# Output stores on another queue, preparation one step further ahead, and a hand-ordered start, in a RetNet-and-ELU kernel

## The chip, the cores and the metric

The kernel runs on one core of a Trainium2 chip. The metric is the device time of one launch in microseconds (us), the median of several executions. Engines in the views: PE (TensorE matmul), PEld (its weight loads), DVE (VectorE), ACT (ScalarE), POOL (GpSimd) and SP (SyncE, which here only issues DMAs). "SPq", "ACTq" and "POOLq" are the queues in which these engines issue DMAs. "PEclk" is the granted PE clock, 1.00 being full speed.

## The reference, cut to what matters

```python
# retention: batch 8, heads 8, sequence 576, head dimension 64
scores = (q @ k.T) / sqrt(64)
Dmat = where(rel >= 0, gamma_h ** rel, 0)      # rel = row - column, one gamma per head
x = ((scores * Dmat) @ v)                      # -> (4608 tokens, 512)
# feed-forward: 512 -> 2048 -> 512
h = x @ w_in
g = where(h > 0, h, exp(min(h, 0)) - 1)        # ELU
out = g @ w_out                                # (4608, 512) float32
```

## The kernel before

Retention works on tiles of 128 rows (and one of 64 at the end of each sequence). A tile is *loaded* (three DMAs: q, k, v), *cast* to bf16 with its decay factors, *turned* (q and k transposed, by PE in the early part and by a DMA transpose later), and put through scores, mask, products and state. The feed-forward part works on nine groups of 512 tokens: `ffn1` makes blocks of hidden units, `ffn2` multiplies them by `w_out`. An instruction given to `pin` keeps its place in program order; one given to `soft` is only pinned while `early[0]` is true.

```python
opool = ctx.enter_context(tc.tile_pool(name="opool", bufs=3))
ps_h  = ctx.enter_context(tc.tile_pool(name="ps_h", bufs=3, space=PSUM))
# ...
    # cast of a full tile, beyond the first batch: both on GpSimd
    soft(nc.gpsimd.tensor_tensor(qkn, rqk, g, ALU.mult))        # 128 x 1024, 1.9 us
    soft(nc.gpsimd.tensor_copy(vn, rv))                         # 128 x 512,  0.6 us
# ...
def ffn1(g, ft, lo=0, n=TG, relu=False):
    # ... four matmuls into ph, a PSUM buffer of ps_h ...
    soft(nc.scalar.activation(e[:, :n], ph[:, :n], AF.Exp))
    if relu:
        soft(nc.scalar.activation(em[:, :n], ph[:, :n], AF.Relu))
        soft(nc.vector.scalar_tensor_tensor(dst, e[:, :n], -1.0, em[:, :n], ALU.add, ALU.min))
    else:
        soft(nc.vector.tensor_scalar_add(em[:, :n], e[:, :n], -1.0))
        soft(nc.vector.scalar_tensor_tensor(dst, ph[:, :n], 0.0, em[:, :n], ALU.max, ALU.min))

def ffn2(g, it, fts, ...):
    # ... when the output tile is complete:
    ot = opool.tile([P, DM], FP32, name="ot", tag="ot")
    soft(nc.scalar.copy(ot, pm))
    pin(nc.sync.dma_start(out[i0 : i0 + P, :], ot))             # behind all loads and transposes on SP

def step():
    s = nxt[0]; nxt[0] += 1
    stretch(s); load(s + 4); cast(s + 2); turn(s + 1)
# ...
for ft in range(NFT):                                           # first 192 tokens of group 1
    ffn1(1, ft, 0, 192)
```

Note the two ways to make the ELU. Without `relu` VectorE runs a `tensor_scalar` (SBUF to SBUF) and a product whose inputs are PSUM and SBUF; with `relu` it runs one product with both inputs in SBUF, and ScalarE does the rest.

## Time and profile before

The time before is 358.93 us in the runs that the prediction had before it. The stage table of the prediction cuts the span at the program's seams:

| stage | what runs | us |
|---|---|---|
| S1, S2 | first tiles; weights arrive; group 0, first half of its outputs | 47.6 |
| S3 | rest of group 0, chains of tiles 4 and 5 | 17.8 |
| S4 | first 192 tokens of group 1 | 16.3 |
| S5 | two chains of tiles | 9.7 |
| S6 | rest of group 1, group 2 begins | 58.3 |
| S7 | steady state | 190.2 |
| S8 | last four output tiles | 17.7 |

### The profile page before, as it was taken

To read this page: it belongs to the slowest core of one execution; us is meant where nothing else is said; L and a number is where in the kernel's file an instruction comes from. 1 tells how busy PE (TensorE), PEld (TensorE's weight loads), DVE (VectorE), ACT (ScalarE), POOL (GpSimd) and SP (SyncE) were. 2 spreads that over 40 slices of the span, in tenths; PEclk is the share of its full clock that TensorE was granted. 3 is DMA by queue.
4 is the path that set the end of the run, shared out by engine and by line. 5 is a ranking of instruction groups with operands and counts; after the bars stand their busy time and mean duration, and the time that the engine had idled before them with its cause. 6 is when DMAs were issued, how large, how long until landed. Compare 5 with 4: busy or idle time off the path is not lost.

```text
span 357.6 us, 6117 instructions
## 1 busy us (share of the span) xinstructions
PE 313.9 (88%) x2319; PEld 161.7 (45%) x2319; DVE 236.3 (66%) x392; ACT 165.7 (46%) x331; POOL 107.1 (30%) x110
## 2 busy tenths in 40 slices
PE   2598983678677995999999999999998999999995
PEld 1443442565444442445444444445544454444442
DVE  3549920675769694967877877778878676666600
ACT  3468511434544562544554555454644455443411
POOL 4356366330255433521332444212234000000000
PEclk9999999559969998999999999999999999999999
DMA  9999999920999959796986896758879320010012
GB/s 172 227 335 332 277 212 232 201 45 18 203 199 199 197 119 205 140 169 141 177 168 136 179 203 132 170 123 186 169 158 140 73 47 29 29 60 29 29 70 78
DMA packets 151484, 53.74 MB, mean 150 GB/s; under 512 B 142752, under 2 KB 142752, under 8 KB 151456
## 3 DMA queue, kind: packets, MB, share of 16 engines
q1 hardware_dynamic: 151456, 53.36, 71.0%
q8 instruction: 18, 0.29, 0.4%
q14 instruction: 10, 0.08, 0.1%
HBM read 36.70 MB, written 9.44 MB: 129 GB/s over the span
## 4 chain that ended last, share of the span: by engine, by line
PE 65%; SPq 12%; DMA 10%; DVE 5%; ACT 4%; issue 2%; POOL 1%; ACTq 0%; POOLq 0%; DVEq 0%
PE pm L71 28%; PE ph L71 27%; SPq L169 10%; DMA qkT<-qkn 6%; PE o L71 4%; PE sc L71 3%; DMA rqk<-in_k_dram 3%; DVE em L324 2%; PE ptr L208 1%; ACT ot L335 1%; SPq L211 1%; DMA out_dram<-ot 1%; DVE g L325 1%; ACT qkT L209 1%; DVE pt L225 1%
## 5 line engine op out<-in xcount | busy, mean ns | idle before, releaser
L71 PE MATMUL ph<-xt,w_in_sb 128*128 128x512 bf16 (+2 forms) x640 | 153.5, 374 | 7.6 <-DVE g L325 5.8
L71 PE MATMUL pm<-w_out_sb,g 128*128 128x512 bf16 x576 | 144.4, 380 | 1.2 <-ACT ot L335 1.1
L317 ACT ACTIVATE e<-ph 128x512 f32<-128x512 f32 (+2 forms) x160 | 88.4, 555 | 93.4 <-PE ph L71 90.1
L324 DVE TENSOR_SCALAR em<-e 128x512 bf16<-128x512 f32 (+2 forms) x156 | 85.8, 552 | 60.7 <-ACT e L317 59.8
L325 DVE SCALAR_TENSOR_TENSOR g<-ph,em 128x512 bf16<-128x512 f32 (+2 forms) x156 | 98.9, 636 | 6.0
L71 PEld LDWEIGHTS <-w_in_sb 128*128 128x128 bf16 x640 | 63.5, 103 | 69.7 <-issue 11.0
L186 POOL TENSOR_TENSOR qkn<-rqk,gtab 128x1024 bf16<-128x1024 f32 x28 | 53.6, 1913 | 118.9 <-DMA rqk<-in_k_dram 92.3
L71 PEld LDWEIGHTS <-g 128*128 128x128 bf16 x576 | 56.4, 98 | 69.4 <-issue 3.2
L225 DVE TENSOR_TENSOR pt<-sc,mask 128x1024 bf16<-128x1024 f32 x32 | 38.9, 1217 | 20.0 <-PE sc L71 20.0
L262 ACT CAST xt<-o 128x512 bf16<-128x512 f32 (+1 forms) x44 | 21.9, 508 | 46.0 <-PE o L71 45.9
L335 ACT COPY ot<-pm 128x512 f32<-128x512 f32 x36 | 21.0, 586 | 34.8 <-PE pm L71 25.2
L71 PE MATMUL sc<-qkT 64*128 64x128 bf16 (+1 forms) x320 | 16.5, 228 | 20.7 <-DMA qkT<-qkn 10.6
L71 PEld LDWEIGHTS <-qkT 64*128 64x128 bf16 x320 | 9.4, 100 | 28.1 <-DMA qkT<-qkn 12.4
L187 POOL CAST vn<-rv 128x512 bf16<-128x512 f32 x28 | 20.0, 713 | 1.5 <-DMA rv<-in_v_dram 1.4
L208 PE MATMUL ptr<-ident,qkn 128*128 128x128 bf16 x64 | 7.1, 270 | 9.0 <-DVE qkn L182 8.0
L71 PE MATMUL o<-pt,vn 128*64 128x128 bf16 x256 | 14.1, 236 | 0.8 <-DVE pt L225 0.8
L192 POOL TENSOR_TENSOR qkt<-rqk,gtab 128x512 bf16<-128x512 f32 x8 | 8.3, 1042 | 21.0 <-DMA rqk<-in_k_dram 21.0
L209 DVE COPY qkT<-ptr 128x512 bf16<-128x512 bf16 x9 | 3.8, 425 | 14.0 <-PE ptr L208 14.0
L143 POOL CAST w_in_sb<-wst 128x512 bf16<-128x512 f32 x13 | 8.9, 689 | 5.9 <-DMA wst<-in_moe_w_in_dram 5.7
L208 PEld LDWEIGHTS <-qkn 128*128 128x128 bf16 x64 | 5.5, 122 | 11.2 <-DVE qkn L182 8.9
L71 PEld LDWEIGHTS <-vn 128*64 128x64 bf16 x256 | 8.7, 115 | 4.1 <-DVE pt L225 0.9
L71 PE MATMUL st<-vn,qkn 128*64 128x64 bf16 x256 | 10.2, 206 | 0.0
(59 smaller groups left out, 113.0 us busy)
## 6 DMA issues: line engine op xcount, KB each, us to landing
out_dram<-ot SPq DMA_DIRECT2D x36, 256.0 KB, 2.2
rqk<-in_q_dram SPq DMA_DIRECT2D x32, 256.0 KB, 4.0
rqk<-in_k_dram SPq DMA_DIRECT2D x32, 256.0 KB, 4.6
rv<-in_v_dram SPq DMA_DIRECT2D x32, 256.0 KB, 4.9
wst<-in_moe_w_in_dram SPq DMA_DIRECT2D x16, 256.0 KB, 5.3
wst<-in_moe_w_out_dram SPq DMA_DIRECT2D x16, 256.0 KB, 5.4
rqk<-in_q_dram SPq DMA_DIRECT2D x8, 128.0 KB, 3.1
rqk<-in_k_dram SPq DMA_DIRECT2D x8, 128.0 KB, 3.5
```

The costliest lines, as they stand in the source:

```text
L71: pin(nc.tensor.matmul(*a, **kw))
L143: soft(engines[eng](w_in_sb[:, j, n * 512 : (n + 1) * 512], t))
L169: pin(nc.sync.dma_start(dst, src[b, :, rows, :].rearrange("h p d -> p h d")))
L186: soft(nc.gpsimd.tensor_tensor(qkn, rqk, g, ALU.mult))
L187: soft(nc.gpsimd.tensor_copy(vn, rv))
L208: pin(nc.tensor.transpose(p[:, hp], flat[:, (i * HP + hp) * P : (i * HP + hp + 1) * P], ident))
L225: soft(nc.vector.tensor_tensor(pt.rearrange("p i h n -> p (i h) n") if n == P else pt, sc.rearrange("p i (h n) -> p (i h) n", h=HP) if n = ...
L262: soft(nc.scalar.copy(xt_tile(g)[:, :, off : off + w], o[:, :, c : c + w]))
L317: soft(nc.scalar.activation(e[:, :n], ph[:, :n], AF.Exp))
L324: soft(nc.vector.tensor_scalar_add(em[:, :n], e[:, :n], -1.0))
L325: soft(nc.vector.scalar_tensor_tensor(dst, ph[:, :n], 0.0, em[:, :n], ALU.max, ALU.min))
L335: soft(nc.scalar.copy(ot, pm))
```

## The change

The intent: loads and transposes should no longer stand behind a store that waits for its output tile; tiles should be prepared earlier; the start should lose the idle time between its chains. The core of the diff:

```diff
-opool = ... bufs=3
+opool = ... bufs=4
 # ffn2
-            pin(nc.sync.dma_start(out[i0 : i0 + P, :], ot))
+            soft(nc.gpsimd.dma_start(out[i0 : i0 + P, :], ot))
 # step
-        load(s + 4)
-        cast(s + 2)
-        turn(s + 1)
+        load(s + 5)
+        cast(s + 3)
+        turn(s + 2)
 # ffn1: nf blocks share one PSUM buffer, one Exp and one mask instruction
-    def ffn1(g, ft, lo=0, n=TG, relu=False):
+    def ffn1(g, ft, lo=0, n=TG, relu=False, nf=1):
 # group 1, first 192 tokens: blocks in pairs, every second pair with relu
-    for ft in range(NFT):
-        ffn1(1, ft, 0, 192)
+    for ft in range(0, NFT, 2):
+        ffn1(1, ft, 0, 192, nf=2, relu=ft % 4 == 2)
 # group 1, other 320 tokens: every second block with relu
-    f1(1, lo=192, n=320)
+    [lambda ft=ft: ffn1(1, ft, 192, 320, relu=ft % 2 == 1) for ft in range(NFT)]
 # start: the loop cast, turn_pe, stretch is written out by hand
-    for s in range(FT):
-        cast(s)
-        ... warm, turn(s, by_pe=True), warm, stretch(s), warm ...
+    cast(0, split=True); turn_pe(0); scores(0); later[0](); state(0)
+    for s in range(1, FT):
+        cast(s, split=True); masks(s - 1); warm(2); turn_pe(s, (0,))
+        inter(s - 1); av(s - 1); turn_pe(s, (1,)); later[s](); warm(1); scores(s)
+        ... state(s) ...
+    ... last_of_start(FT - 1)      # mask, products and copy of the last tile in two halves of head pairs
```

Left out are the helpers that this needs, and the loads, casts and transposes of groups 0 and 1, which are moved one step forward in the same way.

More of the change, by code (lines that the diff above doesn't have):

```diff
@@ L55 @@
     epool = ctx.enter_context(tc.tile_pool(name="epool", bufs=4))
-    opool = ctx.enter_context(tc.tile_pool(name="opool", bufs=3))
+    opool = ctx.enter_context(tc.tile_pool(name="opool", bufs=4))
     ps_h = ctx.enter_context(tc.tile_pool(name="ps_h", bufs=3, space=PSUM))
@@ L148, in w_out_piece @@
         soft(engines[eng](w_out_sb[:, f, :], t))
-    rawt, natt, trt, ptt, ot_ps, st_ps = {}, {}, {}, {}, {}, {}
+    rawt, natt, trt, ptt, ot_ps, st_ps, score_ps = {}, {}, {}, {}, {}, {}, {}
     def size(s):
@@ L170, in load, with cast @@
         rawt[s] = rqk, rv
-    def cast(s):
+    def cast(s, split=False):
         if s >= NS:
@@ L180, in cast @@
             g = gtab[:, t].unsqueeze(3).to_broadcast([P, 2, H, D])
-            if s < FT:
-                pin(nc.vector.tensor_tensor(qkn[:, 0], rqk[:, 0], g[:, 0], ALU.mult))
-                pin(nc.gpsimd.tensor_tensor(qkn[:, 1], rqk[:, 1], g[:, 1], ALU.mult))
-                pin(nc.scalar.copy(vn, rv))
+            if split:
+                soft(nc.vector.tensor_tensor(qkn[:, 0], rqk[:, 0], g[:, 0], ALU.mult))
+                soft(nc.gpsimd.tensor_tensor(qkn[:, 1], rqk[:, 1], g[:, 1], ALU.mult))
+                later[s] = lambda: soft(nc.scalar.copy(vn, rv))
             else:
@@ L194, in cast, with turn_tile, turn, turn_pe @@
         natt[s] = qkn, vn
-    def turn(s, by_pe=False):
-        if s >= NS:
-            return
-        t = s % NT
-        qkn, _ = natt[s]
-        n = 2 * HP if t < FT else HP
-        qkT = tpool.tile([P, n, P], BF16, name="qkT", tag=f"qkT{n}")
-        flat = qkn.rearrange("p i h d -> p (i h d)")
-        if by_pe:
-            for i in range(n // HP):
-                p = ps_h.tile([P, HP, P], BF16, name="ptr", tag="ph")
-                for hp in range(HP):
-                    pin(nc.tensor.transpose(p[:, hp], flat[:, (i * HP + hp) * P : (i * HP + hp + 1) * P], ident))
-                soft(engines["vs"[i]](qkT[:, i * HP : (i + 1) * HP], p))
-        else:
-            pin(nc.sync.dma_start_transpose(qkT, flat))
-        trt[s] = qkT
+    later = {}
+    def turn_tile(s):
+        n = 2 * HP if s % NT < FT else HP
+        trt[s] = tpool.tile([P, n, P], BF16, name="qkT", tag=f"qkT{n}")
+        return n, natt[s][0].rearrange("p i h d -> p (i h d)")
+    def turn(s):
+        if s < NS:
+            _, flat = turn_tile(s)
+            pin(nc.sync.dma_start_transpose(trt[s], flat))
+    def turn_pe(s, parts=(0, 1)):
+        if 0 in parts:
+            turn_tile(s)
+        n = 2 * HP if s % NT < FT else HP
+        flat = natt[s][0].rearrange("p i h d -> p (i h d)")
+        for i in parts:
+            if i * HP >= n:
+                continue
+            p = ps_h.tile([P, HP, P], BF16, name="ptr", tag="ph")
+            for hp in range(HP):
+                pin(nc.tensor.transpose(p[:, hp], flat[:, (i * HP + hp) * P : (i * HP + hp + 1) * P], ident))
+            soft(engines["vs"[i]](trt[s][:, i * HP : (i + 1) * HP], p))
     def scores(s):
@@ L222, in scores, with masks @@
                 mm(sc[:, i, hp * n : (hp + 1) * n], kT[r, hp], qkT[r, hp, :n], start=True, stop=True)
+        score_ps[s] = sc
+    def masks(s):
+        n = size(s)
+        sc = score_ps.pop(s)
         pt = ppool.tile([P, 2, HP, n], BF16, name="pt", tag=f"pt{n}")
@@ L233, in scores, with inter @@
         ptt[s] = pt
-    def inter(s):
+    def inter(s, only_tile=False):
         b, t = divmod(s, NT)
@@ L239, in inter @@
         ot_ps[s] = o
-        if t:
+        if t and not only_tile:
             for hp in range(HP):
@@ L280, in state, with last_of_start @@
         soft(nc.scalar.copy(sb[D:, :, D:], st[D:]))
+    def last_of_start(s):
+        sc = score_ps.pop(s)
+        vn = natt.pop(s)[1]
+        g, off = divmod(s * P, TG)
+        xt = xt_tile(g)
+        o = ot_ps.pop(s)
+        o2 = ps_h.tile([P, HP, P], FP32, name="o2", tag="ph")
+        pt = ppool.tile([P, 2, HP, P], BF16, name="pt", tag="pt128")
+        half = HP // 2
+        for a in range(2):
+            hs = slice(a * half, (a + 1) * half)
+            soft(nc.vector.tensor_tensor(
+                pt[:, :, hs], sc.rearrange("p i (h n) -> p i h n", h=HP)[:, :, hs],
+                mask.unsqueeze(1).unsqueeze(1).to_broadcast([P, 2, half, P]), ALU.mult,
+            ))
+            oo = (o, o2)[a]
+            for hp in range(a * half, (a + 1) * half):
+                mm(oo[:, hp], sbd[(s - 1) % 2][:, hp], trt[s][:, hp], start=(hp == a * half), stop=False,
+                   skip_group_check=True)
+            for hp in range(a * half, (a + 1) * half):
+                for i in range(2):
+                    h = 2 * hp + i
+                    mm(oo[i * D : (i + 1) * D, hp], vn[:, h], pt[:, i, hp], start=False, stop=True,
+                       skip_group_check=True)
+            soft(engines["sv"[a]](xt[:, hs, off : off + P], oo[:, hs]))
+        del trt[s]
     def stretch(s):
@@ L287, in stretch @@
             scores(s)
+            masks(s)
         if late:
@@ L308, in gtile @@
         return gts[g, ft]
-    def ffn1(g, ft, lo=0, n=TG, relu=False):
+    def ffn1(g, ft, lo=0, n=TG, relu=False, nf=1):
         xt = xt_tile(g)
         ph = ps_h.tile([P, TG], FP32, name="ph", tag="ph")
-        for j in range(KJ):
-            mm(ph[:, :n], w_in_sb[:, j, ft * P : (ft + 1) * P], xt[:, j, lo : lo + n],
-               start=(j == 0), stop=(j == KJ - 1))
         e = epool.tile([P, TG], FP32, name="e", tag="e")
-        soft(nc.scalar.activation(e[:, :n], ph[:, :n], AF.Exp))
-        dst = gtile(g, ft)[:, lo : lo + n]
         em = epool.tile([P, TG], BF16, name="em", tag="em")
+        for f in range(nf):
+            for j in range(KJ):
+                mm(ph[:, f * n : (f + 1) * n], w_in_sb[:, j, (ft + f) * P : (ft + f + 1) * P],
+                   xt[:, j, lo : lo + n], start=(j == 0), stop=(j == KJ - 1))
+        m = n * nf
+        soft(nc.scalar.activation(e[:, :m], ph[:, :m], AF.Exp))
         if relu:
-            soft(nc.scalar.activation(em[:, :n], ph[:, :n], AF.Relu))
-            soft(nc.vector.scalar_tensor_tensor(dst, e[:, :n], -1.0, em[:, :n], ALU.add, ALU.min))
-        else:
-            soft(nc.vector.tensor_scalar_add(em[:, :n], e[:, :n], -1.0))
-            soft(nc.vector.scalar_tensor_tensor(dst, ph[:, :n], 0.0, em[:, :n], ALU.max, ALU.min))
+            soft(nc.scalar.activation(em[:, :m], ph[:, :m], AF.Relu))
+        else:
+            soft(nc.vector.tensor_scalar_add(em[:, :m], e[:, :m], -1.0))
+        for f in range(nf):
+            c = slice(f * n, (f + 1) * n)
+            dst = gtile(g, ft + f)[:, lo : lo + n]
+            if relu:
+                soft(nc.vector.scalar_tensor_tensor(dst, e[:, c], -1.0, em[:, c], ALU.add, ALU.min))
+            else:
+                soft(nc.vector.scalar_tensor_tensor(dst, ph[:, c], 0.0, em[:, c], ALU.max, ALU.min))
     def ffn2(g, it, fts, pool=None, tag="pm"):
@@ L354 @@
         load(s)
-    for s in range(FT):
-        cast(s)
-        last = s == FT - 1
-        warm(4 * last)
-        turn(s, by_pe=True)
-        warm(last)
-        stretch(s)
-        warm(3 * last)
-    finish(FT - 1)
-    warm(3)
+    cast(0, split=True)
+    turn_pe(0)
+    scores(0)
+    later[0]()
+    state(0)
+    for s in range(1, FT):
+        cast(s, split=True)
+        masks(s - 1)
+        warm(2)
+        turn_pe(s, (0,))
+        inter(s - 1)
+        av(s - 1)
+        turn_pe(s, (1,))
+        later[s]()
+        warm(1)
+        scores(s)
+        if s < FT - 1:
+            state(s)
+    warm(2)
+    inter(FT - 1, only_tile=True)
+    qkn3, vn3 = natt[FT - 1]
+    last_of_start(FT - 1)
+    natt[FT - 1] = qkn3, vn3
     for i in range(6):
@@ L369 @@
         ffn1(0, ft, relu=ft % 2 == 1)
+        if ft == 0:
+            state(FT - 1)
+            natt.pop(FT - 1)
         while n_in < min(16, 2 * ft + 8):
@@ L387 @@
         ffn2(0, 2, part)
-    turn(FT, by_pe=True)
+    turn_pe(FT)
     stretch(FT)
-    cast(FT + 1)
+    cast(FT + 1, split=True)
     for part in Q:
         ffn2(0, 3, part)
-    turn(FT + 1, by_pe=True)
+    turn_pe(FT + 1)
+    later[FT + 1]()
     stretch(FT + 1)
     finish(FT + 1)
+    early[0] = False
     cast(FT + 2)
-    early[0] = False
     load(FT + 5)
-    for ft in range(NFT):
-        ffn1(1, ft, 0, 192)
-        if ft == 7:
-            turn(FT + 2, by_pe=True)
+    load(FT + 6)
+    for ft in range(0, NFT, 2):
+        ffn1(1, ft, 0, 192, nf=2, relu=ft % 4 == 2)
+        if ft == 8:
+            turn_pe(FT + 2)
             stretch(FT + 2)
             cast(FT + 3)
-            load(FT + 6)
+            load(FT + 7)
     for i, part in enumerate(Q):
@@ L408 @@
         if i == 2:
-            turn(FT + 3, by_pe=True)
+            turn_pe(FT + 3)
             stretch(FT + 3)
             cast(FT + 4)
-            load(FT + 7)
-    turn(FT + 4, by_pe=True)
+            load(FT + 8)
+    turn_pe(FT + 4)
     stretch(FT + 4)
@@ L418 @@
     cast(FT + 6)
-    load(FT + 8)
+    turn(FT + 6)
+    cast(FT + 7)
+    load(FT + 9)
     nxt = [FT + 5]
@@ L444, in f2 @@
         return [lambda it=it, p=p: ffn2(g, it, p) for it in its for p in Q]
-    run([[x] for x in f1(1, lo=192, n=320) + f2(1, (1,))], last_step(2) + 1)
+    a = [lambda ft=ft: ffn1(1, ft, 192, 320, relu=ft % 2 == 1) for ft in range(NFT)]
+    run([[x] for x in a + f2(1, (1,))], last_step(2) + 1)
     a, c = f1(2), f2(1, (2, 3))
```

## The prediction

> **What bounds the kernel now.** I read four views of the profile of before: the busy shares, the stage table (busy time of each engine in windows that I cut at the program's own seams), the order of time, and the wait table. The first two say that there are two kernels in one.
>
> ```profile
> PE 313.9 (88%) x2319; PEld 161.7 (45%) x2319; DVE 236.3 (66%) x392; ACT 165.7 (46%) x331; POOL 107.1 (30%) x110
> ```
> ```profile
> 0.00:24.07 24.07, 13.24 (x152) 8.69 (x152) 11.22 (x31) 11.83 (x25) 9.96 (x22) 1.00 1.11 240
> 24.07:47.62 23.55, 21.79 (x97) 9.29 (x96) 18.83 (x32) 15.26 (x29) 12.50 (x18) 1.00 0.91 287
> 47.62:65.39 17.77, 10.06 (x88) 5.47 (x88) 2.77 (x4) 3.68 (x8) 10.43 (x9) 0.88 1.05 225
> 65.39:81.64 16.25, 12.96 (x89) 10.62 (x88) 12.56 (x31) 6.27 (x18) 6.64 (x6) 0.50 0.53 102
> 81.64:91.29 9.65, 7.52 (x103) 4.85 (x100) 4.44 (x8) 4.84 (x12) 0.00 (x0) 1.00 0.15 43
> 91.29:149.63 58.34, 46.98 (x420) 25.70 (x420) 44.49 (x71) 27.54 (x61) 26.01 (x22) 0.91 1.05 185
> 149.63:339.86 190.23, 187.41 (x1314) 90.98 (x1313) 141.67 (x217) 93.93 (x177) 41.56 (x35) 1.00 0.60 121
> 339.86:357.60 17.74, 13.97 (x64) 6.13 (x63) 0.35 (x1) 2.34 (x4) 0.00 (x0) 1.00 0.20 75
> ```
>
> Columns: window, its length, busy time (count) of PE, PE weight loads, DVE, ACT and POOL, granted PE clock, DMA share, GB/s. Call the rows S1 to S8. S7 and S8 are PE-bound: 2.8 us idle in S7, and S8 is 64 matmuls back to back and a tail. Nothing there is to be won. S1 to S6 take 149.6 us, with 36 us of PE idle and, in S4, a clock of 0.50. That is where the change works, so each stage is priced by itself.
>
> The wait table, for the queue that issues all DMAs, and the order of time say why:
>
> ```profile
> SPq L337 <- ACT ot L335: 141.2, 33, 16.9
> ```
> ```profile
> 56.68 5.27 SPq L337 DMA_DIRECT2D out_dram<-ot  x4
> 61.01 0.58 ACT L335 COPY ot<-pm 128x512 f32<-128x512 f32 x1 [9.16 <-DMA out_dram<-ot]
> 62.14 0.61 PE L71 MATMUL sc<-qkT 64*128 64x128 bf16 x8 [5.75 <-ACT qkT L209]
> ```
> ```profile
> 70.09 1.13 SPq L169 DMA_DIRECT2D rv<-in_v_dram  x1
> 88.16 0.36 SPq L337 DMA_DIRECT2D out_dram<-ot  x1
> ```
>
> First line: waited for, us in total, times, longest. The second block is the hole in S3. Four stores stand behind fifteen loads in one in-order queue; the fourth output copy on ACT needs one of three `ot` buffers, waits 9.16 us for a store to land, and the `qkT` copy behind it on ACT holds PE 5.75 us. The third block is the hole that S6 pays for: the queue does nothing from 71.2 to 88.2 us, because the next store waits for its `ot`; the loads behind it come 18 us late, and PE then waits for transposes in S6 (3.44, 0.42, 1.02 and 3.78 us are the largest gaps).
>
> [...] No run here shows the GpSimd queue yet. [...] after the 5.75 us gap the clock of S4 is 0.50, and eight transposes take 1.14 us there against 0.61 in S5. [...] a 128x192 tensor_scalar takes 0.24 us alone and 1.73 beside a 1.90 us cast on POOL.
>
> **The change part by part.**
>
> *S1 and S2, start.* Before, the mask of tile 2 (1.22 us) stood ahead of the q cast of tile 3 on DVE. That cast ended at 19.5 us, though the k cast ended at 17.3. Now the cast goes first. From 17.3 us: transposes 0.4 to 0.6, copy 0.58, scores 0.5, half a mask about 0.65, products 0.4, half-size copy 0.4, and waits between: the first `ph` at about 21.5 instead of 24.07, 2.5 us earlier. But S2 ends when the last weight piece has come: it is cast on POOL at 45.29 to 45.9, having just landed, and before used it at about 46.4. DMA is at 0.88 to 1.00 there, 353 GB/s at its best, so the weights hardly come sooner; 1 us if the third `w_in` piece is no longer stuck on ACT until 23.91. **S1+S2: 47.6 to 46.6.** Most of the hand pipelining is hidden behind the weight stream.
>
> *S3.* From 47.62 to 55.66 as before, 8.0 us; transposes and the copy of `qkT` without the store wait, 1.4; then the chain scores, mask, products, copy, 3.25 us as before (62.14 to 65.39), less some 0.4 for the full clock. **17.8 to 12.2.** The 9.16 us wait falls because the stores go out as soon as each copy is there, and there are four buffers.
>
> *S4.* [...] PE needs 64 matmuls of 192 columns; at 0.216 us for 512 columns (20 pairs of S7) that is about 5.3, so DVE sets the pace. Pairs of blocks now share instructions: tensor_scalar over 384 about 0.36 (0.25 at 192, 0.33 at 320), two products at 0.36: 1.08 a pair; the relu pairs lose the tensor_scalar but their products have two SBUF inputs (0.82 against 0.69 at 512): 0.9 a pair. 4 x 1.08 + 4 x 0.9 = 7.9, plus a `qkT` copy 0.42 and a mask 1.22: 9.6. One or two collisions with POOL casts: **16.25 to 11.0.**
>
> *S5.* Chains of turn, scores, products at full clock already: 9.65, unchanged.
>
> *S6.* PE work at full clock: 46.98 busy, less about 4.5 that the half clock after two gaps cost (about 9 us of work at half speed), is 42.5. DVE is near it in the first 20 us: 16 blocks of 320 at 0.82 now alternate with relu ones. If all tiles came in time this would be 45. They do not quite: see the first rival. I take **58.3 to 49.**
>
> *S7.* 2.8 us of idle, mostly for transposes one step ahead; two steps ahead should take most: **190.2 to 188.5.**
>
> *S8.* [...] **17.7 to 18.5.**
>
> Sum: 46.6 + 12.2 + 11.0 + 9.65 + 49 + 188.5 + 18.5 = 335.4 of span. Before, the median is 1.3 above the profiled span (358.93 against 357.6): **336.8, say 337 us**, a gain of 6%.
>
> **The rivals.**
>
> *DMA becomes the bound in S6.* When the queue is backed up, a tile's three loads take 3 x 1.1 us to issue and a transpose 2.04 (median), 5.4 us for a full tile, while a step of PE in S6 needs 4 to 6. Before could load only 5 tiles by 71 us and then stood. After still has a hole: in the built order of POOL the store of the first output tile of group 1 stands ahead of the cast of tile 10; that store waits for its copy, at about 76 us, and the transpose of tile 10 and the loads behind it on SP wait too. For it: DMA share of 1.05 in S6. Against: S6 before took 58 us for the same transfers with two more waits for stores in it. It would make S6 54 to 56 and the time 342 to 344.
>
> *POOL becomes the new queue that blocks.* 36 stores wait in order on POOL, now in front of casts[...]. Against: POOL is 30% busy,[...] and the casts run three steps ahead. For: any late cast delays SP's loads. 3 to 8 us in S6 and S7: 340 to 345.
>
> *The start is worth its full 2.5 us*, if the weights are not the bound: 335.5.
>
> **Range and chances.** The gains of S3 and S4, 10.8 us, stand on waits that the trace names, and I trust them to 3 us. S6's 9 us may be anything from 3 to 13. The two first rivals overlap and push up, so the range is wider there: **331 to 345 us**. Faster by over 2% means below 351.8, which needs S6 to give nothing and S4 to lose half as well: 0.95 faster, 0.04 within 2%, 0.01 slower.
>
> **What would show it.** In the profile of after: the first `ph` at 21 to 22 us but the end of the first two output tiles of group 0 near 46.5 (start hidden by the weights; if it is near 44.5, I was wrong there). No ACT wait on `out_dram<-ot` of more than 1 us, and no PE gap over 3 us between 50 and 80 us; granted clock 1.0 from 60 to 80. `ph` of 192 columns taking 10 to 12 us, with DVE over 80% busy. In S6, waits of PE for `qkT` of 2 to 6 us in sum; over 8 is the first rival. Waits of POOL stores for `ot` in the wait table, and casts behind them: long ones with PE idle are the second rival. The prediction is wrong if the clock drops again between 55 and 75, or if S7 grows past 192 us.

The sum came to 335.4 us of span, 336.8 us of time. All its terms still stand, but the reasons of two are among the cuts: that S4 runs at full clock (in its 11.0 us), and why a last store from GpSimd makes S8 0.8 us longer (in its 18.5 us). These two were estimates. Before had no store on GpSimd; without the 0.8 the sum would be 334.6. Of the second rival, its 3 to 8 us were an estimate too.

## More of the kernel before

One view that the prediction does not show is needed for the comparison: who made PE wait in S6. These are the two largest lines of PE's waits in that window (who waits, for whom, us in total, times, longest):

```profile
PE sc L71 <- DMA qkT<-qkn: 8.7, 4, 3.8
PE ph L71 <- DVE g L325: 2.6, 3, 1.9
```

Before, S6 waits for transposed tiles that come late, and hardly for VectorE.

## The result, and the profile after

The first four executions of the changed kernel took 340.85 to 345.66 us, median **343.82**, beside 359.47 for the kernel before on the same chip: ratio 0.956 (95% interval 0.947 to 0.964). A later set of six (`e10_again`, below) gave 342.04. A ratio is always the mean time of one kernel's fast runs over that of the other's of the same rounds, so not quite the ratio of the quoted medians. "Slow" for a kernel on one core means only that a run was over 1.5% above the fastest of its kernel. There is no second group of times: the runs of one kernel spread over 0.7 to 2.8%, roughly in step with the granted clock. The kernel before spreads over 0.5 to 1.2% within a set.

The stage table of the profiled run after (345.34 us), rows S1 to S8 in the columns of the prediction's table:

```profile
0.00:20.53 20.53, 11.73 (x141) 7.37 (x144) 10.83 (x32) 10.47 (x22) 7.92 (x19) 1.00 1.12 217
20.53:48.34 27.81, 22.02 (x105) 9.49 (x105) 18.76 (x33) 16.03 (x31) 13.11 (x19) 1.00 0.95 297
48.34:60.53 12.19, 9.44 (x88) 5.08 (x89) 4.08 (x5) 4.21 (x9) 9.92 (x11) 1.00 1.00 262
60.53:72.66 12.13, 8.61 (x88) 7.69 (x89) 9.04 (x20) 5.69 (x13) 4.92 (x6) 0.86 1.07 211
72.66:82.10 9.44, 7.25 (x98) 4.75 (x99) 4.27 (x8) 5.39 (x13) 2.79 (x3) 1.00 0.48 96
82.10:136.25 54.15, 44.95 (x415) 25.16 (x420) 47.06 (x62) 29.87 (x69) 30.38 (x26) 0.97 1.24 206
136.25:324.12 187.87, 185.88 (x1289) 90.98 (x1312) 138.88 (x218) 94.03 (x177) 54.21 (x59) 1.00 0.57 117
324.12:343.60 19.48, 13.92 (x63) 6.17 (x63) 0.35 (x1) 2.34 (x4) 2.71 (x5) 0.96 0.18 68
```

Against the prediction: S3 hits (12.2), S7 is 0.6 better, S1 and S2 together are 1.7 worse (48.3 against 46.6, and even later than before), S4 is 1.1 worse, S6 5.2 worse, S8 1.0 worse. With 0.2 less in S5 that makes the 8.15 us by which the span, 343.6, is above the predicted 335.4. S6 is nearly two thirds of it. PE's largest waits in S6 are now:

```profile
PE ph L71 <- DVE g L372: 8.1, 6, 2.4
PE ph L71 <- ACT xt L274: 0.5, 1, 0.5
```

The 8.7 us for transposed tiles are gone, all of them. In their place PE waits 8.1 us for `g`, the ELU product on VectorE: the wait changed its name. Its origin is in the order of time (start, length, engine, instruction; in brackets the idle time before it and who ended it):

```profile
79.24 0.58 POOL L384 DMA_DIRECT2D out_dram<-ot  x1 [11.88 <-ACT ot L382]
79.89 1.89 POOL L186 TENSOR_TENSOR qkn<-rqk,gtab 128x1024 bf16<-128x1024 f32 x1
...
84.83 2.25 POOL L186 TENSOR_TENSOR qkn<-rqk,gtab 128x1024 bf16<-128x1024 f32 x1
85.23 2.03 DVE L365 TENSOR_SCALAR em<-e 128x320 bf16<-128x320 f32 x1
87.84 1.25 PE L71 MATMUL ph<-xt,w_in_sb 128*128 128x320 bf16 x8 [1.62 <-DVE g L372]
87.91 1.91 POOL L186 TENSOR_TENSOR qkn<-rqk,gtab 128x1024 bf16<-128x1024 f32 x1 [0.18 <-DMA rqk<-in_k_dram]
88.30 1.86 DVE L370 SCALAR_TENSOR_TENSOR g<-e,em 128x320 bf16<-128x320 f32 x1
```

Read it from the top. GpSimd reaches the first store of group 1 and stands still for 11.88 us, until ScalarE has made that output tile. It is the longest of many such waits in the wait table of GpSimd over the whole span (us in total, times, longest):

```profile
POOL out_dram L384 <- ACT ot L382: 134.6, 31, 11.9
```

The casts that stand behind it then run one after the other, beside the ELU blocks. A `tensor_scalar` of 320 columns, 0.32 us when nothing runs beside it, takes 2.03 us beside a 2.25 us cast; a product with two SBUF inputs, 0.48 us alone, takes 1.86 us. PE waits for the results.

There is a second surprise, in S4. It has no PE gap over 3 us, and yet the granted clock falls:

```profile
66.07 0.61 PE L218 MATMUL ptr<-ident,qkn 128*128 128x128 bf16 x8 [1.62 <-DVE g L372]
68.22 0.40 PE L71 MATMUL sc<-qkT 64*128 64x128 bf16 x8 [1.55 <-DVE qkT L219]
...
68.80 3.81 PE L71 MATMUL ph<-xt,w_in_sb 128*128 128x192 bf16 x24
```

Twenty-four matmuls of 192 columns took 2.14 us at the start of S4 and take 3.81 here. Finer windows give PEclk 1.00 up to 69.0, 0.54 from 69.0 to 69.5 and 0.50 from 69.5 to 72. From 64.45 to 68.22 us, 3.77 us, PE ran nothing but eight transposes, 0.61 us; both gaps are under 1.7 us. So what comes before the halved clock here is not one long gap but some microseconds with little work for PE. How little, and for how long, lowers the clock is not shown.

### The profile page after: what moved, and what is told of

Read it like the earlier page. It is cut to its first block, busy times and chain, and to the rows that moved or that the text cites. A ratio compares the mean times of both kernels' runs of the same rounds, so it can differ in the third digit from the quotient of the medians.

```text
span 343.6 us, 6072 instructions
## 1 busy us (share of the span) xinstructions
PE 303.8 (88%) x2281; PEld 156.7 (46%) x2319; DVE 233.3 (68%) x375; ACT 168.0 (49%) x336; POOL 125.9 (37%) x145
## 4 chain that ended last, share of the span: by engine, by line
PE 42%; issue 28%; DVE 14%; SPq 4%; DMA 4%; POOL 4%; ACT 3%; POOLq 0%; ACTq 0%; DVEq 0%
PE pm L71 18%; PE ph L71 18%; DVE em L365 5%; DMA wst<-in_moe_w_in_dram 4%; DVE g L372 4%; SPq L169 4%; PE o L71 3%; DVE g L370 3%; POOL out_dram L384 2%; PE sc L71 2%; DVE pt L237 2%; POOL qkn L186 1%; ACT e L361 1%; SPq L142 1%; ACT xt L274 1%
## 5 line engine op out<-in xcount | busy, mean ns | idle before, releaser
L71 PE MATMUL ph<-xt,w_in_sb 128*128 128x512 bf16 (+2 forms) x620 | 147.5, 363 | 16.1 <-DVE g L372 8.1
L71 PE MATMUL pm<-w_out_sb,g 128*128 128x512 bf16 x560 | 141.6, 379 | 2.2 <-ACT ot L382 1.1
L361 ACT ACTIVATE e<-ph 128x512 f32<-128x512 f32 (+2 forms) x152 | 87.1, 575 | 91.8 <-PE ph L71 86.3
L365 DVE TENSOR_SCALAR em<-e 128x512 bf16<-128x512 f32 (+2 forms) x136 | 77.4, 569 | 58.8 <-ACT e L361 58.7
L372 DVE SCALAR_TENSOR_TENSOR g<-ph,em 128x512 bf16<-128x512 f32 (+2 forms) x140 | 92.2, 661 | 5.8
L71 PEld LDWEIGHTS <-w_in_sb 128*128 128x128 bf16 x640 | 60.6, 99 | 75.4 <-issue 16.7
L384 POOL DMA_DIRECT2D out_dram<-ot x36 | 20.4, 567 | 137.4 <-ACT ot L382 134.6
L186 POOL TENSOR_TENSOR qkn<-rqk,gtab 128x1024 bf16<-128x1024 f32 x27 | 52.3, 1936 | 18.7 <-PE st L71 10.3
L187 POOL CAST vn<-rv 128x512 bf16<-128x512 f32 x27 | 18.3, 678 | 28.5 <-PE o L71 19.6
L370 DVE SCALAR_TENSOR_TENSOR g<-e,em 128x192 bf16<-128x192 f32 (+2 forms) x20 | 15.5, 791 | 2.9 <-ACT em L363 2.7
```

The lines of the kernel that those rows point to most:

```text
L71: pin(nc.tensor.matmul(*a, **kw))
L361: soft(nc.scalar.activation(e[:, :m], ph[:, :m], AF.Exp))
L365: soft(nc.vector.tensor_scalar_add(em[:, :m], e[:, :m], -1.0))
L370: soft(nc.vector.scalar_tensor_tensor(dst, e[:, c], -1.0, em[:, c], ALU.add, ALU.min))
L372: soft(nc.vector.scalar_tensor_tensor(dst, ph[:, c], 0.0, em[:, c], ALU.max, ALU.min))
L384: soft(nc.gpsimd.dma_start(out[i0 : i0 + P, :], ot))
```

## The experiments

Theory A, after this reading: what the prediction missed in S4 and S6 is how much longer VectorE's `tensor_scalar` (0.32 to 2.03 us above) and two-SBUF-input products (0.48 to 1.86 us) take beside GpSimd's casts. Rivals: (B) the waiting store on GpSimd itself is the cause; (C) DMA is the limit, and whatever is taken away returns as another wait; (D) the further lookahead is what brought the gain, and the store move did little, or the reverse.

Twelve kernels were run, in three sets of four, the first two sets on one chip and the third (`e10_again`, `e11_stores_sp`, `e12_one_less_act`, `e13_no_pair`) on another. So kernels of different sets are compared by their ratios. Each was timed six times beside runs of the kernel before (medians of the sets: 359.84, 360.34 and 359.72 us). All gave right results. Stages are from the profiled run of each:

| kernel | median us | ratio to before (95%) | S1+S2 | S3 | S4 | S5 | S6 | S7 | S8 |
|---|---|---|---|---|---|---|---|---|---|
| before | 359.8 | 1 | 47.6 | 17.8 | 16.3 | 9.7 | 58.3 | 190.2 | 17.7 |
| changed, first profile | 343.82 | 0.956 (0.947–0.964) | 48.3 | 12.2 | 12.1 | 9.4 | 54.2 | 187.9 | 19.5 |
| e10_again: changed, repeated | 342.04 | 0.949 (0.945–0.954) | 48.2 | 12.2 | 12.0 | 9.9 | 50.6 | 187.9 | 19.5 |
| e2_stores_only | 352.26 | 0.978 (0.974–0.981) | 48.7 | 12.2 | 17.9 | 9.7 | 55.9 | 187.9 | 19.5 |
| e1_old_start | 340.38 | 0.945 (0.940–0.949) | 47.5 | 12.2 | 10.0 | 9.7 | 54.1 | 187.9 | 19.5 |
| e4_no_lock | 336.32 | 0.934 (0.931–0.938) | 48.7 | 12.2 | 9.4 | 9.7 | 48.7 | 187.9 | 19.5 |
| e7_one_store | 341.15 | 0.939 (0.934–0.944) | 47.3 | 12.2 | 13.5 | 9.7 | 51.3 | 187.9 | 19.5 |
| e3_stores_act | 339.20 | 0.946 (0.939–0.952) | 46.3 | 12.9 | 9.8 | 9.9 | 47.5 | 187.9 | 17.7 |
| e5_win_pool | 344.58 | 0.956 (0.950–0.963) | 45.8 | 12.2 | 14.0 | 9.9 | 50.5 | 187.9 | 19.5 |
| e6_one_less | 340.31 | 0.948 (0.942–0.953) | 48.2 | 12.2 | 9.6 | 9.7 | 50.4 | 187.9 | 19.6 |
| e9_all_new | 334.74 | 0.931 (0.928–0.934) | 48.4 | 12.7 | 10.3 | 9.7 | 47.6 | 188.2 | 17.8 |
| e11_stores_sp | 338.36 | 0.937 (0.932–0.943) | 49.0 | 12.2 | 8.1 | 9.7 | 49.0 | 187.9 | 17.8 |
| e13_no_pair | 349.62 | 0.970 (0.965–0.975) | 48.3 | 12.2 | 15.6 | 11.3 | 53.8 | 187.9 | 19.5 |
| e12_one_less_act | 336.63 | 0.936 (0.932–0.940) | 47.3 | 12.7 | 10.8 | 9.9 | 47.0 | 187.9 | 17.7 |

One thing to keep beside the table: the two profiles of the *same* changed kernel have S6 at 54.2 and 50.6 us. A difference in S6 of less than 4 us between two profiles is no verdict alone. The same goes for two other columns. S1 and S2 together lie between 46.3 and 49.0 us in the nine profiles with the start and the weight casts of the changed kernel. S4 lies between 9.6 and 14.0 us in the six profiles with its matmuls, its ELU forms and all or nearly all stores on GpSimd (the changed kernel twice, `e1_old_start`, `e5_win_pool`, `e6_one_less`, `e7_one_store`).

### e2_stores_only: the kernel before, with only the stores moved (and the fourth buffer)

```diff
-    opool = ... bufs=3
+    opool = ... bufs=4
-            pin(nc.sync.dma_start(out[i0 : i0 + P, :], ot))
+            soft(nc.gpsimd.dma_start(out[i0 : i0 + P, :], ot))
```

> The kernel before with only its stores moved to the GpSimd queue (and four ot buffers). Theory: the in-order wait of the stores is the main loss, so this part alone brings most of the gain: S3 about 12.3 us, clock of S4 near 1.0 and S4 about 13, S6 about 55, S8 19.5, time about 348.5 us. Rival: the gain comes from the extra step of lookahead and the rebuilt stages; then this run stays at 354 us or more.

Measured: 352.26 us, between the two (whether it is 2% faster than the kernel before stays unclear). The hole in S3 is gone to the tenth (12.18), and so are all waits for transposed tiles in S6; but S4 does not fall, it rises to 17.9 us at a mean clock of 0.71. The order of time shows why:

```profile
60.88 1.91 POOL L186 TENSOR_TENSOR qkn<-rqk,gtab 128x1024 bf16<-128x1024 f32 x1
61.80 4.05 DVE L324 TENSOR_SCALAR em<-e 128x192 bf16<-128x192 f32 x1 [2.04 <-ACT e L317]
62.73 0.60 POOL L187 CAST vn<-rv 128x512 bf16<-128x512 f32 x1
63.30 1.89 POOL L186 TENSOR_TENSOR qkn<-rqk,gtab 128x1024 bf16<-128x1024 f32 x1
65.14 0.60 POOL L187 CAST vn<-rv 128x512 bf16<-128x512 f32 x1
...
66.31 0.80 PE L71 MATMUL ph<-xt,w_in_sb 128*128 128x192 bf16 x4 [4.24 <-DVE g L325]
```

One instruction of 0.24 us took 4.05 us, until 65.85. Beside it ran four GpSimd instructions, two casts of q and k and the two of v behind them, which followed each other without a gap. PE stood 4.24 us. So the expectation that S4 recovers once the hole in S3 is gone was wrong: the hole is gone, and the clock of S4 is 0.71.

### e4_no_lock: no VectorE instruction in group 1 that can collide

```diff
+            if g == 1:
+                soft(nc.scalar.activation(em[:, :m], e[:, :m], AF.Identity, bias=neg1))   # e - 1 on ScalarE
             # group 1 then takes the product with inputs in PSUM and SBUF, never tensor_scalar
```

> The changed kernel with the minus one of group 1 on ACT (exp, then identity with bias -1), so that DVE has only products with one SBUF input in the narrow blocks, which should not collide with POOL. Theory[...]: products stay at 0.36 and 0.49 us beside casts, S6 49 to 50, S4 11 to 12, time 338 to 340. Rival, DVE is full by its own work: this takes away some 2.5 us of own work (8 x 0.31), time about 341.5; the products would be as long beside casts as the ops they replace.

Measured: 336.32 us; S4 9.4 at a clock of 1.00, S6 48.7. The forms of VectorE instructions in S6 (busy us, mean ns, idle before) of the changed kernel, then of this one:

```profile
L370 DVE SCALAR_TENSOR_TENSOR g<-e,em 128x320 bf16<-128x320 f32 x8 | 7.1, 884 | 0.6 <-ACT em L363 0.5
L365 DVE TENSOR_SCALAR em<-e 128x320 bf16<-128x320 f32 x8 | 5.9, 737 | 3.1 <-ACT e L361 3.1
L372 DVE SCALAR_TENSOR_TENSOR g<-ph,em 128x320 bf16<-128x320 f32 x8 | 3.9, 490 | 0.2
```
```profile
L377 DVE SCALAR_TENSOR_TENSOR g<-ph,em 128x320 bf16<-128x320 f32 x16 | 7.7, 490 | 8.1 <-ACT em L366 8.1
```

The product with one PSUM input has a mean of 490 ns in both, with casts beside it or not (in the changed kernel at most 492 ns in either case); the means of the other two forms, 737 and 884 ns, are about twice their length alone, 0.32 and 0.48 us. VectorE spends 7.7 us on group 1 in place of 16.9. Theory A holds, and the rival of the expectation (VectorE full by its own work, 341.5 us) falls. The stage figures alone would lie within the scatter, but the times do not: the ratio's interval, 0.931 to 0.938, is clear of the changed kernel's. Not all of PE's wait for `g` is gone: 4.8 us of it stay in S6, of which 3.0 before the 320-column blocks, whose products now wait for ScalarE (8.1 us in the last line). This run moves no store and makes no transfer earlier, so C falls as the main cause, and B can be one only by way of the collisions (see `e11_stores_sp`).

### e7_one_store: only the store that stands 11.88 us goes to another queue

```diff
-            soft(nc.gpsimd.dma_start(out[i0 : i0 + P, :], ot))
+            soft((nc.scalar if (g, it) == (1, 0) else nc.gpsimd).dma_start(out[i0 : i0 + P, :], ot))
```

> The changed kernel with one store alone (first tile of group 1) issued by ACT, all orders on the other engines as they were. Theory: that store holds the casts of tiles 10 to 13 on POOL for 11.9 us and bunches them into the stage where DVE is full[...]; without it they run from about 68 us on, the 320-column tensor_scalar falls from 0.74 to under 0.5 us, S6 from 54.2 to about 50, time 339.5 to 340.5. Rival 1, DMA is the bound of S6: PE waits for qkT appear or S6 stays at 54. Rival 2, DVE is full by its own work: S6 stays at 54, time 343 to 344.

Measured: 341.15 us; three of its six runs count as slow, among them the profiled one. PE's wait for `g` in S6 was 5.6 us in place of 8.1, but the second profile of the unaltered kernel has 5.8. S4 took 13.5 us. All of this is within the scatter, and the profile is of a slow run, so this run settles nothing.

### e1_old_start: the hand-ordered start undone

```diff
-    cast(0, split=True); turn_pe(0); ...; last_of_start(FT - 1)
+    for s in range(FT): cast(s, split=True); later[s](); ... turn_pe(s) ... stretch(s) ...
```

> The changed kernel with the start of the kernel before (tile by tile, mask ahead of the next cast, last tile whole). Theory: the start is hidden behind the weight stream, so S1 goes back to 24.0 us and S2 back to about 23.5, sum 47.6 against 48.3 now, and the time is 343 to 344.5 us, no worse than the changed kernel. Rival: the hand pipelining is worth its 2.5 to 3.5 us; then 346.5 to 347.5.

Measured: 340.38 us; the ratio's interval (0.940 to 0.949) overlaps that of the changed kernel (0.945 to 0.954). The first `ph` is 3.1 us later (23.63 against 20.53), and S1 and S2 together are 47.5 against 48.3. The hand-ordered start starts earlier and ends no earlier: it is worth nothing that these runs can see.

### e5_win_pool: the weight casts away from ScalarE

```diff
-        w_in_piece(i, "ppsppp"[i])            # p: GpSimd, s: ScalarE
+        w_in_piece(i, "p")
-            w_in_piece(n_in, "pspp"[n_in % 4])
+            w_in_piece(n_in, "p")
```

> The changed kernel with all casts of the pieces of w_in on GpSimd instead of ScalarE. Theory: in S2 ScalarE stands 2.66 us before a cast of a weight piece that has not landed, and the gate work behind it waits; without these casts S1 and S2 together fall from 48.3 to about 46.5 us, and the time to 341.5 to 342.5 us. Rival (the pieces themselves land late, whoever casts them): S1 and S2 together stay at 48 us or more and the time at 343 to 345 us, as the casts also lengthen VectorE's instructions.

Measured: S1 and S2 take 45.8 us in the profile, 2.5 less, and ScalarE no longer stands before a piece of `w_in`. That the one comes from the other is not shown: `e3_stores_act`, with the weight casts untouched, has 46.3 us, and `e9_all_new`, with the same edit as here, has 48.4. The time is 344.58, not lower. S4 took 14.0 us at a clock of 0.77 in the profiled run, with a `tensor_scalar` of 384 columns (0.35 us alone) stretched to 3.67 us beside two casts and those of v behind them. In this profile, S4 took back what S2 gave.

### e6_one_less: lookahead back by one step

```diff
-        load(s + 5); cast(s + 3); turn(s + 2)
+        load(s + 4); cast(s + 2); turn(s + 1)      # and the loads of groups 0 and 1 likewise
```

> The changed kernel with the casts, transposes and loads back at one step less of lookahead, everything else as changed. Theory (the further step is what took away the waits for transposed tiles in S6): PE waits for the transposed tiles come back in S6 and the start of S7, 3 to 5 us, and the time is 347 to 348 us. Rival (the stores moved off SyncE had already done that): no such wait of more than 1 us, and the time stays at 343 to 344 us.

Measured: 340.31 us, and no wait of PE for a transposed tile in S6. The theory falls: once the stores are off SyncE, the extra step brings nothing that these runs can see (ratio 0.948 against 0.949 for the changed kernel).

### e10_again and e11_stores_sp: the changed kernel, and the changed kernel with its stores back on SyncE

> The changed kernel again, unaltered, so that the other runs of this set can be compared with it in the same rounds. The first four runs gave 340.9 to 345.7 us. If the time with one step less of lookahead (340.3 us) is really lower, this stays near 343 to 344 us; if the two are the same, it comes out at 340 to 341 us.

```diff
-            soft(nc.gpsimd.dma_start(out[i0 : i0 + P, :], ot))
+            pin(nc.sync.dma_start(out[i0 : i0 + P, :], ot))
```

> The changed kernel with the stores back on the SyncE queue, all else as changed. Theory (the moved stores are what removed the hole in S3 and the waits for transposed tiles in S6, and the further lookahead is no substitute): S3 back at about 17.8 us, PE waits for transposed tiles of 2 us or more in S6, S8 back to 17.7; 343.8 + 5.6 + 2 to 4 - 1.7 = 350 to 352 us. Rival (the lookahead alone hides the queue behind a waiting store): S3 stays near 12 us, no such waits, about 342 us.

Measured in the same rounds: 342.04 us for the changed kernel, between the two readings of its expectation, and **338.36** with the stores *back*. My theory expected 350 to 352. Undoing the part that gives the change its name made it faster by 3.7 us (338.36 / 342.04 = 0.989; the intervals of the two ratios, 0.932 to 0.943 and 0.945 to 0.954, do not overlap). And S3 did not grow. Lines of the order of time, with the stores back on SyncE:

```profile
57.19 0.59 ACT L382 COPY ot<-pm 128x512 f32<-128x512 f32 x1 [4.01 <-PE pm L71]
57.67 2.80 SPq L384 DMA_DIRECT2D out_dram<-ot  x4
...
72.41 1.92 POOL L186 TENSOR_TENSOR qkn<-rqk,gtab 128x1024 bf16<-128x1024 f32 x1
75.71 0.36 SPq L384 DMA_DIRECT2D out_dram<-ot  x1
76.26 1.90 POOL L186 TENSOR_TENSOR qkn<-rqk,gtab 128x1024 bf16<-128x1024 f32 x1 [1.38 <-DMA rqk<-in_k_dram]
```

The first two lines explain S3. All four stores still stand behind the loads and go out from 57.67 us, no earlier than before (56.68). But the fourth copy has already been made, at 57.19, ahead of every store: it found a *fourth buffer*, where the kernel before waited 9.16 us for one of its three to be emptied. By this trace the one-character edit `bufs=4` is enough to remove the hole, with the stores where they were (the earlier loads of the change are in this run too). The moved stores look to be enough as well: in the changed kernel the first two go out from 48.61 us and land within 5.5 us, so for the copy at 56.59 a buffer was free even out of three.

The rest bears on S6. The queue of SyncE now stands only from 73.1 us (the end of its last load) to 75.71, because S3 and S4 are shorter and one tile more is loaded first; before, it stood from 71.2 to 88.2. And GpSimd is not held by a store: it casts at 72.4 and 76.3, during S5, where VectorE runs masks and copies of chains and PE does not wait for ELU blocks. PE's largest waits in S6 are

```profile
PE sc L71 <- DMA qkT<-qkn: 3.9, 3, 2.1
PE ph L71 <- DVE g L372: 0.8, 1, 0.8
```

3.9 us for transposed tiles come back, as expected, but of the waits for VectorE 0.8 us is left, where the repeat profile of the changed kernel has 5.8. S8 is 17.75 again in place of 19.54. So rival B has its share after all: the store held on GpSimd is upstream, and the collisions of theory A are how it reaches PE. Rival D is half right: the moved stores alone take away all waits for late tiles in S6 (`e2_stores_only`, `e6_one_less`), the further lookahead alone leaves 3.9 of the 8.7 us.

The largest difference between the two profiles is in another stage: S4 takes 8.1 us here and 12.0 in the repeat of the changed kernel, 3.9 of the 6.8 us between the spans. Here the cast that begins at 60.77 us is over at 62.67, before the first pair of products with two SBUF inputs (63.55, 0.63 us), and the clock stays at 1.00; in the first profile of the changed kernel a cast at 62.02 lies across that pair, which takes 1.98 us. Whether the queue of the stores sets when this cast comes, or chance, is not shown.

### e3_stores_act: stores on ScalarE's queue

```diff
-            soft(nc.gpsimd.dma_start(out[i0 : i0 + P, :], ot))
+            soft(nc.scalar.dma_start(out[i0 : i0 + P, :], ot))
```

> The changed kernel with every output store issued on the ScalarE queue instead of the GpSimd queue. Theory: in the changed kernel the first store of group 1 stands ahead of a cast and holds GpSimd for 11.9 us, and a store from GpSimd lands 1.0 us later than one from SyncE; with ScalarE issuing them (it has produced the tile, so it waits for nothing) the casts come earlier and stage S6 falls from 54.2 to about 51 us, S8 from 19.5 to about 18, and the time from 343.8 to 340 to 341 us. Rival (the stores cost nothing where they are[...]): S6 stays at 54, only S8 shrinks, 342.5 to 344 us.

Measured: 339.20 us (three of the six runs count as slow, as the fastest, which is the profiled one, took 333.6); S8 is 17.74 as the theory has it, and S6, at 47.5, is lower still than its 51. The median does not differ for certain from the changed kernel's: the ratio intervals overlap. One reason that I gave is refuted: the median store from ScalarE also needs 3.2 us to land, as from GpSimd, and S8 is short all the same.

### e13_no_pair: the 192-column blocks one by one

```diff
-    for ft in range(0, NFT, 2):
-        ffn1(1, ft, 0, 192, nf=2, relu=ft % 4 == 2)
-        if ft == 8:
+    for ft in range(NFT):
+        ffn1(1, ft, 0, 192, relu=ft % 4 > 1)
+        if ft == 9:
```

> The changed kernel with the 192-column blocks of group 1 no longer worked in pairs (a pair shares one Exp and one mask instruction), the share of blocks with the mask on ScalarE as in the changed kernel. Theory (pairing shortened S4 by taking instructions, and their exposure to GpSimd, off VectorE and ScalarE): S4 rises from 12.1 to 15 to 18 us, time 347 to 350 us. Rival (S4 is set by matmul work and the clock once the stores are gone): S4 stays at 11 to 13 us and the time at 343 to 344 us.

Measured: 349.62 us, **7.6 us slower** than the changed kernel in the same rounds; S4 15.6 at a clock of 0.67, S5 11.3 at 0.85. So a part that the change's short description doesn't name is the largest gain that any of these runs takes back. By the profiles 3.6 us of it lie in S4 and 1.4 in S5; the 3.2 of S6 are within its scatter. How S4 begins, first in the changed kernel, then here:

```profile
60.53 2.14 PE L71 MATMUL ph<-xt,w_in_sb 128*128 128x192 bf16 x24 [0.68 <-ACT xt L274]
```
```profile
60.51 1.15 PE L71 MATMUL ph<-xt,w_in_sb 128*128 128x192 bf16 x12 [0.68 <-ACT xt L274]
63.49 0.80 PE L71 MATMUL ph<-xt,w_in_sb 128*128 128x192 bf16 x4 [1.83 <-DVE g L372]
```

There are three `ps_h` buffers. With a pair in each, PE runs 24 matmuls (six blocks) before it must wait for VectorE; with one block in each it runs 12. The same collision with a cast (a `tensor_scalar` of 1.65 us at 61.40) then leaves PE idle for 1.83 us, and the four matmuls after it take 0.80 us, where twelve had taken 1.15: PEclk is 1.00 from 60 to 62 us, 0.58 from 62 to 64 and 0.50 from 64 to 68. From 60 to 62 us PE was busy for 1.15 us, from 62 to 64 for 0.51. Pairs save instructions, which the prediction counted, and also give PE twice the work to live on, which it did not.

### e9_all_new and e12_one_less_act: the repairs together

`e9_all_new` is the changed kernel with `e - 1` on ScalarE in group 1 and every second block of group 2, stores on ScalarE's queue and `w_in` cast on GpSimd. `e12_one_less_act` has the edits of `e6_one_less`, `e4_no_lock` and `e3_stores_act`.

> The changed kernel with all repairs at once: one of the two mask subtractions moved from VectorE to ScalarE in group 1 and in every second block of group 2, stores on the ScalarE queue, and w_in cast on GpSimd. Theory (the parts add up, as they sit in different stages): S1 and S2 together 46.5, S4 9.4, S6 46, S8 18, so 331 to 332 us. Rival (ScalarE, with the subtractions and the stores, becomes what PE waits for in S6, or the earlier casts collide elsewhere): 335 us or more, no better than the subtractions moved alone (336.3).

> The changed kernel with one step less of lookahead, the stores on the ScalarE queue, and the mask subtraction of group 1 on ScalarE; w_in cast as in the changed kernel. If the gains add: S4 9.5, S6 47.5 to 48.5, S8 17.7, S1 and S2 together 47 to 48.5, so 333 to 335 us, level with or better than all repairs with the full lookahead (334.7). If earlier casts without the further lookahead leave transposed tiles late now that ScalarE is busier: PE waits for them, 337 us or more.

Measured: 334.74 and 336.63 us; their intervals overlap with each other and with that of `e4_no_lock`. By its median `e9_all_new` is the fastest kernel, 6.9% under the kernel before, but 3 us over what adding the parts promised. The terms that fell short, in its profile: S1 and S2 together took 48.4 us (46.5 expected), S4 10.3 at a clock of 0.83 (9.4 expected), S6 47.6 (46 expected); S8 came as expected (17.8). S3 took 12.7 to 12.9 in all three kernels with stores on ScalarE, 0.5 to 0.7 more than in the others. The gain of `e5_win_pool` in S2 did not repeat. `e12_one_less_act` came out between its two readings: PE waits only 0.3 us for a transposed tile in S6, and the term that fell short is S4, 10.8 us at a clock of 0.87 (9.5 expected).

## Why the prediction was right or wrong

The time was inside the range, near its upper end: 337.0 predicted, 331 to 345 the range, 343.82 measured (342.04 in the later set). Of the 22 us promised, 15.7 came, 17.7 in the later set. The mechanism was right in S3, S7 and the hidden start, and wrong in S4 and S6. By a sign of its own ("wrong if the clock drops again between 55 and 75") the prediction fails: the clock was 0.50 from 69.0 to 72.4 us. Both of its first rivals named times that hold the measured one (342 to 344 and 340 to 345), so the time alone does not speak for the main text.

A few readings in it are off, and none decides: PE's idle time in S1 to S6 is 37.1 us and not 36; S6 giving nothing and S4 half would end near 349 us and not at 351.8; and the profiled run of before took 359.51, 1.9 us above its span and not 1.3.

- **Start (S1 and S2, 46.6 predicted).** Right that it is hidden, and the first `ph` came at 20.5, near the 21 to 22 named as a sign. Wrong by 1.7 us in the end: the extra 1 us "if the third `w_in` piece is no longer stuck on ACT" did not come. ScalarE now waits 2.66 us before another piece, but that this wait sets the end of S2 is not shown: `e5_win_pool` and `e9_all_new` both take it away and end at 45.8 and 48.4.
- **S3 (12.2 predicted, 12.19 measured).** The number is exact. The text gave two reasons together: the stores go out early, *and* there are four buffers. By the traces one of them is enough: `e11_stores_sp` has only the second and keeps all of S3's gain, and in the changed kernel the first stores have landed before a fourth buffer is needed.
- **S4 (11.0 predicted, 12.1 and 12.0 measured).** The failing step is the full clock that the text takes for S4 (its sign, "granted clock 1.0 from 60 to 80"). The clock fell to 0.50 after gaps of 1.62 and 1.55 us, in which PE waited for VectorE, each time after two products with two SBUF inputs had taken long there beside casts, 1.98 and 1.73 us (0.63 in `e11_stores_sp`, after the cast was over). I had counted that as "one or two collisions" of a fixed length. The pairing was priced as VectorE work; `e13_no_pair` shows 7.6 us of time for it. `e2_stores_only` shows that the hole in S3 had not been the only cause of the slow S4.
- **S6 (49 predicted, 54.2 and 50.6 measured).** This is the mis-sized term. The sum took "PE work at full clock", 42.5, which holds (43.1 us of PE in `e11_stores_sp`, whose S6 has a clock of 1.00), and "If all tiles came in time this would be 45", which does not. All tiles did come in time (no wait for `qkT`, where the sign said 2 to 6 us), and S6 was still 5.6 to 9.2 us above 45. What stood in their place was the wait for VectorE, 8.1 us in the first profile and 5.8 in the second. With the collisions of group 1 taken out, S6 is 48.7. The first rival had the right event, the store of group 1 ahead of a cast in the built order of POOL, but the wrong way for it to hurt: not through late transfers, through casts that run in a bunch beside the ELU blocks. The second rival called POOL a queue that blocks. Its sign was there, stores on POOL that wait (134.6 us in all) with casts behind them, and the stores there do cost 3.7 us of time (`e11_stores_sp`), 1.8 of them in S8 and none in S7.
- **S7 (188.5 predicted, 187.9 measured).** Right in size. The step named, "two steps ahead", is not needed: with the stores moved and one step less (`e6_one_less`) it is 187.87, with the stores on SyncE and the further step 187.87, and with the stores alone moved (`e2_stores_only`) 187.86. Either suffices, with the fourth buffer, which all these runs have.
- **S8 (18.5 predicted, 19.5 measured).** Right in sign. The loss is 1.8 us and not 0.8; with stores on SyncE or ScalarE it is zero. The tail, from the end of the last output copy to the end of the span, is 4.84 us in the changed kernel and 3.11 with the stores on SyncE. A later start of the issue (0.28) and a later landing (2.3 us after that start against 2.0) make 0.6 of the 1.7 us of difference; the rest comes after the landing. There, in the trace of the changed kernel, GpSimd runs a DRAIN instruction of 3.8 us (the views of the profile leave such instructions out), which ends at 342.86 us, 1.5 us after the last store has landed, and its closing semaphore instructions follow that. In the trace of the kernel before, no DRAIN of GpSimd at the end takes over 0.1 us.

What stays open. No run has the fourth buffer alone, or the moved stores with three buffers, so what each does for S3 and S7 rests on the traces. No run takes away the relu form alone. No run has the stores on SyncE *without* the further lookahead beside the pairing. `e11_stores_sp` with `e - 1` on ScalarE was not run either; it might beat 334.74. What sets the end of S2 is not known.

## What to carry to other kernels

A wait for an output buffer (9.16 us here) can be mended with one more buffer; look at which of several edits in a bundle is doing that before crediting the largest. Before moving DMAs onto an engine that also computes, ask what stands behind them in its order: here a store that waited for its tile held GpSimd for 11.88 us, and when it let go, the casts behind it ran in a bunch, in the stage that was then on. Where VectorE and GpSimd overlap, measure VectorE's instructions beside the other's and price them at that length (2.03 us for 0.32 here), or try forms with a PSUM input (0.49 us either way here), and give PE enough buffered work to outlast a collision (24 matmuls in place of 12 here; without the pairs the kernel was 7.6 us slower).
